# Weight units in fourths behind the last k and q tiles, five units in halves, and Sinkhorn's column sums as two 256-column products

## The chip, the cores and the metric

One core of a Trainium2 chip runs the whole program; the other cores are idle. The metric is the device time of one execution in microseconds (us), the median of several runs. TensorE (PE in the profile) multiplies matrices, VectorE (DVE), ScalarE (ACT) and GpSimd (POOL) do the rest, and SyncE (SP) issues most of the transfers. A transfer is issued by an engine's instruction stream, in the order of that stream, and moved by 16 DMA engines.

## What is computed

Three layers follow each other: a linear attention with 8 heads, a soft mixture of 8 experts with 32 slots, and a mixture of 8 experts whose gate is balanced by eight Sinkhorn steps. Everything is float32, with 2304 tokens of 512 features.

```python
# attention, per head, S = 576 rows, 128 random features
phi(x): p = x @ w_phi; p = p - max|p|;  [exp(p), exp(-p)]
num = phi(q) @ (phi(k).T @ v);  den = phi(q) @ sum(phi(k));  x = num / (den + 1e-6)
# first mixture: N = 2304 tokens, 8 experts x 4 slots, hidden 1024
slot_input = softmax(x @ phi, over tokens).T @ x
slot_out[e] = relu(slot_input[e] @ w1[e]) @ w2[e]
x = softmax(x @ phi, over slots) @ slot_out
# second mixture: 8 experts
P = exp(x @ w_gate - max)
for _ in range(8):
    P /= P.sum(1) + 1e-9
    P /= P.sum(0) + 1e-9        # the column sums: over all 2304 tokens
    P *= N / E
out = sum over e of P[:, e] * (relu(x @ w1[e]) @ w2[e])
```

## The kernel before

The tokens stand in 18 tiles of 128 rows (NT = 18). The program has three stages.

**Attention.** A loop over i runs 25 times; the k side works on tile i, the q side on tile t = i - 7. `k_project` and `q_project` multiply a k or q tile of 256 KB with w_phi and then issue the load of the tile four ahead (`load_k`, `load_q`, lines 134 and 155) on SP, into buffers of four that belong to the pools `kp` and `qtp`. From the 14th tile on there is no tile four ahead and nothing is loaded into a buffer that comes free.

**First mixture.** Its weights are 32 units of 1 MB (`units`, line 111): unit 4e + n is half n of w1 of expert e, unit 4e + 2 + n is half n of w2. In the trace and in the orders below, a unit is named by expert and half, so unit 4 is `moe_w_1_0`, unit 21 `moe_w_5_1` and unit 28 `moe_w_7_0`. Twelve units are loaded in quarters during the k loop (`attn_units`, line 495). When the k side is done its pool is closed, and in its room six more units (19 to 23 and 26) are loaded in halves by `load_part` from ACT's stream: `halves` (line 620) is the list, and each of the iterations from i = 18 takes one behind the logits and two between the exponentials. Unit 4 is loaded whole into a pool of its own (`wk1`, line 633) once the q tiles are done; units 5, 6, 10, 16 and 7 follow in halves when the q side's pool is closed (lines 678 to 682). Then the experts run in four pairs p: `up` multiplies with w1, `turn` transposes, `down` multiplies with w2. As a unit is used up its buffer takes the next load (lines 899 to 944): 17, 24, 28, 29, 25, 27, 30, 31 and the four units of the second mixture's first expert. `make_stack(0)` (line 991) is the first work that needs the last two of these.

**Second mixture.** For each expert nine blocks of 256 tokens run (`for i, (e, blk)`, line 1247). A block has 8 products of the first layer (`first_layer`) and 7 Strassen products of 12 matmuls each, all 256 columns wide; hidden values and weights are split in a rounded part and a remainder, both of the type fp32r. Beside the blocks of expert 0, `sinkhorn` (line 1021) is a generator that is advanced five times in a block: after product 1 three times, after product 5 twice. In each of its eight rounds VectorE sums P over the tiles (`cs`), TensorE sums over the partitions with one product of ones and `cs`, 8 columns wide and in float32 (line 1067, `pcs` in the trace), and VectorE divides. The column sum over the tiles is made after product 5, `pcs` runs after product 1 of the next block.

The order on each engine is the order in which the program is written (`InOrder`, line 43). Pools are stacks of memory: a pool opened where another was closed waits for the last use of the tiles it covers.

Of the kernel before, what the change touches and what calls it, by code (L numbers as in the profile page):

```python
# [54 lines left out]
def tile_kernel(ctx: ExitStack, tc: tile.TileContext, a):  # L55
# [31 lines left out]

    def w1_unit(name, e, n):
        t = unit_t[name, e, n]
        if isinstance(t, list):  # L90
            return t
        return [t[:, k * FF:(k + 1) * FF] for k in range(2)]
# [22 lines left out]
    qp = qstack.enter_context(tc.tile_pool(name="qp", bufs=2, side="left"))  # L115
    qtp_cm = tc.tile_pool(name="qtp", bufs=4, side="left")
    qtp = qtp_cm.__enter__()
    kp = kstack.enter_context(tc.tile_pool(name="kp", bufs=2, side="right"))
# [15 lines left out]
    def load_k(t):  # L134
        x = kp.tile([128, 512], F32, tag="kt", name=f"kt{t}", bufs=4)
        SP.dma_start(out=x, in_=a["kT"][t])
        kt_t[t] = x
# [48 lines left out]
    def k_project(t, banks):  # L186
        project("k", kt_t.pop(t), t, banks)
        if t + 4 < NT:
            load_k(t + 4)

# [42 lines left out]
    def q_project(t, banks):  # L233
        project("q", qt_t.pop(t), t, banks)
        if t + 4 < NT:
            load_q(t + 4)
        if t:
            q_shift(t)
# [238 lines left out]
    const.tile([128, 8], F32, name="pad", bufs=1)  # L477
# [53 lines left out]

    K0, K1, X, Q0, Q1 = "ABECD"
    for i in range(NT + LAG):
# [9 lines left out]
        if 0 <= t:  # L543
            q_num(t, 0, X)
            if i in attn_units:
                load_part(*attn_units[i], 0, 4)
            if t + 1 == NT:
                slot_dd(3, P1)
                run_exps()
                most = first.tile([128, 1, NS], F32, tag="gm", name="most", bufs=1)  # L550
                V.tensor_copy(out=most.rearrange("p o j -> p (o j)"), in_=run["mb"][:, 0:NS])
                q_divide_last(t, 0)
            q_num(t, 1, Q0)
        if i >= NT and t + 1 < NT:
            x_logits(t - 1, Q1)
        if i in attn_units:
            load_part(*attn_units[i], 1 if t >= 0 else 0, 4)
        if i >= NT and halves:
            load_part(*halves.pop(0), 2)
        if i < NT:  # L560
# [55 lines left out]
            if i + 1 == NT:  # L616
                kstack.close()
                wk_cm = tc.tile_pool(name="wk", bufs=6, side="right", reuse_waits="tile")
                wk = wk_cm.__enter__()
                halves = [(wk, u, h) for u in (19, 20, 21, 22, 23, 26) for h in range(2)]  # L620
                F0, U0, U1, P0, P1 = Q1, X, Q0, K0, K1
                X, Q0, Q1 = F0, U0, U1
# [8 lines left out]
        if t + 3 == NT:  # L631
            qtp_cm.__exit__(None, None, None)
            wk1_cm = tc.tile_pool(name="wk1", bufs=1, side="right", reuse_waits="tile")
            wk1 = wk1_cm.__enter__()
            load_units(wk1, 4)
        if t + 1 < NT:
            for hh in range(2):
                q_transpose(t + 1, hh, (F0, U1)[hh])
                q_exp(t + 1, hh)
                if halves:  # L640
                    load_part(*halves.pop(0), 2)
# [255 lines left out]
    for n in range(4):  # L897
# [3 lines left out]
        if n == 2:  # L901
            load_units(wk1, 28)
# [3 lines left out]
    for p in range(E // 2):  # L906
# [39 lines left out]
        if p == 1:  # L946
            wq_cm.__exit__(None, None, None)
            early_cm.__exit__(None, None, None)
# [8 lines left out]
    next(slot_turns)  # L957
    next(slot_splits)
    w_lo(0, 3, V)
# [10 lines left out]
    wk1_cm.__exit__(None, None, None)  # L970
    wk_cm.__exit__(None, None, None)
    wb_cm.__exit__(None, None, None)
# [48 lines left out]
    def sinkhorn():  # L1021
# [32 lines left out]
        yield  # L1054
        for it in range(8):
# [8 lines left out]
            V.tensor_reduce(out=csf, in_=P.rearrange("p t e -> p e t"), axis=AX.X, op=ALU.add)  # L1064
            yield
            pg = z_tile(0, f"pcs{it}") if it < 7 else acc_tile(f"pcs{it}")
            PE.matmul(pg[:, 0:E], ones, csf, start=True, stop=True)
# [274 lines left out]
```

## Time and profile before

| | us |
|---|---|
| median of 3 runs | 994.38 |
| lowest and highest run | 990.32, 995.48 |
| the profiled execution, its own time | 995.96 |
| span of the profile (first to last instruction) | 994.1 |

Shares of the span: PE 99 % busy, DVE 69 %, POOL 60 %, ACT 56 %. The trace gives, for each instruction, engine, start, duration and the idle time before it with what ended it. "PEld" is the loading of a matmul's stationary operand, which overlaps the matmuls. All instructions of helpers have line 51, so rows are read by the names of the tiles. Ends of matmuls are modelled: the distance between the starts of two is what they cost. A row ending in x12 merges 12 instructions.

### The profile page before, as it was taken

How to read it: one execution, taken by the hardware profiler on the slowest of the kernel's cores; microseconds unless marked ns; L12 is line 12 of the kernel's file. 1: busy time of each engine (PE TensorE's matmuls, PEld its weight loads, DVE VectorE, ACT ScalarE, POOL GpSimd, SP SyncE). 2: the span in 40 equal slices, each digit the busy share in tenths (PEclk: the TensorE clock that was granted, in tenths of full speed). 3: DMA queues.
4: the chain of work that ended last, by engine and by line, in shares of the span. 5: the costliest groups of instructions: out<-in, count | busy, mean ns of one | idle time of the engine just before them, and what ended most of it. 6: DMA issues, size and time to landing. Idle time of an engine off the chain costs nothing.

```text
span 994.1 us, 28051 instructions
## 1 busy us (share of the span) xinstructions
PE 980.6 (99%) x11698; PEld 935.7 (94%) x11698; DVE 688.8 (69%) x1360; ACT 556.5 (56%) x1018; POOL 593.7 (60%) x462
## 2 busy tenths in 40 slices
PE   8899999999999999999999999999999999999998
PEld 7899987569999999999999999999999999999998
DVE  6778766277886766676766776676676677667675
ACT  5566554265657666655564555554654565555452
POOL 2122220055678677867786678678777777787443
PEclk9999999999999999999999999999999999999999
DMA  8777578980003100310040004000400130001111
GB/s 238 219 239 221 170 244 301 393 303 2 1 1 128 44 1 1 128 44 2 1 156 16 1 1 170 2 2 20 151 2 1 66 106 1 2 1 38 49 44 64
DMA packets 29517, 88.84 MB, mean 89 GB/s; under 512 B 3920, under 2 KB 6864, under 8 KB 24144
## 3 DMA queue, kind: packets, MB, share of 16 engines
q1 hardware_dynamic: 20560, 68.05, 20.0%
q10 hardware_dynamic: 8640, 18.88, 5.9%
q8 instruction: 92, 1.51, 0.6%
q14 instruction: 33, 0.27, 0.1%
q0 software_dynamic: 192, 0.13, 0.1%
HBM read 82.33 MB, written 4.72 MB: 88 GB/s over the span
## 4 chain that ended last, share of the span: by engine, by line
PE 96%; DMA 1%; DVE 1%; issue 1%; ACT 1%; DVEq 0%; ACTq 0%
PE x L51 39%; PE y L51 20%; PE z L51 16%; PE kvacc L51 4%; PE num L51 3%; PE pq L51 2%; PE pk L51 2%; PE ut L51 2%; DMA moe_w<-in_moe_w 1%; PE ps L51 1%; PE ph L51 1%; PE po L51 1%; PE xt L51 1%; PE lg L51 1%; PE xl L51 1%
## 5 line engine op out<-in xcount | busy, mean ns | idle before, releaser
L51 POOL TENSOR_TENSOR hl_s<-s,hh_s 128x512 fp32r<-128x512 f32 x286 | 365.5, 1300 | 205.7 <-ACT hh_s L51 189.6
L51 PE MATMUL x<-w_t,hh_s 128*128 128x256 f32 x1152 | 204.7, 278 | 0.1
L51 ACT ACTIVATE hh_s<-s 128x512 fp32r<-128x512 f32 x287 | 174.9, 630 | 50.6 <-PE x L51 26.3
L51 ACT ACTIVATE r<-z 128x512 f32<-128x512 f32 x143 | 85.8, 600 | 163.0 <-PE z L51 162.3
L51 PEld LDWEIGHTS x<-w_t,hh_s 128*128 128x128 f32 x1152 | 173.4, 188 | 1.1 <-ACT xo L51 0.3
L51 DVE SCALAR_TENSOR_TENSOR xo<-x,P,xo 128x256 f32<-128x256 f32 x252 | 120.9, 480 | 68.3 <-PE x L51 66.7
L51 ACT ACTIVATE hh_a<-z 128x512 fp32r<-128x512 f32 x216 | 122.2, 600 | 73.2 <-DVE s L51 71.7
L51 PE MATMUL x<-w_t,hl_s 128*128 128x256 f32 x576 | 158.7, 276 | 0.0
L51 DVE SCALAR_TENSOR_TENSOR s<-z,r 128x512 f32<-128x512 f32 x143 | 98.0, 685 | 84.6 <-ACT hh_a L51 80.7
L51 DVE SCALAR_TENSOR_TENSOR hl_a<-z,hh_a 128x512 fp32r<-128x512 f32 x216 | 147.1, 681 | 2.7 <-ACT hh_a L51 2.7
L51 PEld LDWEIGHTS x<-w_t,hl_s 128*128 128x128 f32 x576 | 107.9, 188 | 0.0
L51 PE MATMUL z<-w_b,hh_a 128*128 128x256 f32 x576 | 102.4, 278 | 0.0
L51 PE MATMUL y<-w_b,hh_s 128*128 128x256 f32 x576 | 101.7, 276 | 0.0
L51 PE MATMUL x<-w_t,hh_a 128*128 128x256 f32 x576 | 101.6, 276 | 0.0
L51 PE MATMUL y<-w_t,hh_s 128*128 128x256 f32 x576 | 101.6, 276 | 0.0
L51 PE MATMUL x<-w_b,hh_a 128*128 128x256 f32 x576 | 101.3, 276 | 0.0
L51 DVE SCALAR_TENSOR_TENSOR s<-z,s 128x512 f32<-128x512 f32 x143 | 97.7, 684 | 3.9 <-POOL hl_s L51 2.1
L51 PEld LDWEIGHTS z<-w_b,hh_a 128*128 128x128 f32 x576 | 86.6, 188 | 2.9 <-issue 2.9
L51 PEld LDWEIGHTS y<-w_b,hh_s 128*128 128x128 f32 x576 | 86.8, 188 | 0.0
L51 PEld LDWEIGHTS x<-w_t,hh_a 128*128 128x128 f32 x576 | 86.8, 188 | 0.0
L51 PEld LDWEIGHTS y<-w_t,hh_s 128*128 128x128 f32 x576 | 86.8, 188 | 0.0
L51 PEld LDWEIGHTS x<-w_b,hh_a 128*128 128x128 f32 x576 | 86.6, 188 | 0.0
(211 smaller groups left out, 1982.7 us busy)
## 6 DMA issues: line engine op xcount, KB each, us to landing
moe_w<-in_moe_w SPq DMA_DIRECT2D x41, 1024.0 KB, 6.9
moe_w<-in_moe_w ACTq DMA_DIRECT2D x48, 256.0 KB, 3.7
moe_w<-in_moe_w ACTq DMA_DIRECT2D x12, 512.0 KB, 5.3
vs<-in_vb SPq DMA_DIRECT2D x20, 256.0 KB, 4.2
kt<-in_kT SPq DMA_DIRECT2D x18, 256.0 KB, 4.1
qt<-in_qT SPq DMA_DIRECT2D x18, 256.0 KB, 3.4
half<-in_moe_w SPq DMA_DIRECT2D x8, 512.0 KB, 6.6
out<-xo SPq DMA_DIRECT2D x18, 128.0 KB, 1.7
```

Source lines behind the costliest of these rows:

```text
L51: return lambda *args, **kwargs: self.tc.keep_in_program_order(make(*args, **kwargs))
```

## The change

It has three parts.

- **Weight units.** The k tiles get a pool of their own (`ktp`) that stays open, and the pool of the q tiles (`qtp`) moves below the q side's and stays open too. Behind the last four k tiles come the four fourths (256 KB each) of unit 4, behind the last four q tiles the fourths of unit 21, and later, in the same buffers as unit 4, the fourths of unit 28. All are issued by SP. `Columns` makes two fourths look like one tile. The pool `wk1` is gone, `wk` has 5 buffers instead of 6, and `halves` holds five units (20, 19, 22, 23, 26), taken four times per iteration instead of three.
- **Column sums.** VectorE rounds `cs` to fp32r (`csh`) and takes the remainder (`gst`), and TensorE multiplies ones of the type fp32r with both, each repeated 32 times to 256 columns, in one accumulation.
- **One VectorE instruction.** `w_lo(0, 3, V)` stands ahead of the last `slot_splits` instead of behind it.

```diff
+    def load_fourth(pool, tag, u, m):
+        name, e, n = units[u]
+        t = pool.tile([128, 512], F32, tag=tag, name=f"{name}_{e}_{n}_{m}")
+        SP.dma_start(out=t, in_=a[name][e, :, n * 2048 + m * 512:n * 2048 + (m + 1) * 512])
+        unit_t.setdefault(units[u], []).append(t)
...
-    qp = qstack.enter_context(tc.tile_pool(name="qp", bufs=2, side="left"))
     qtp_cm = tc.tile_pool(name="qtp", bufs=4, side="left")
     qtp = qtp_cm.__enter__()
+    qp = qstack.enter_context(tc.tile_pool(name="qp", bufs=2, side="left"))
+    ktp_cm = tc.tile_pool(name="ktp", bufs=4, side="right")
+    ktp = ktp_cm.__enter__()
...
         if t + 4 < NT:
             load_k(t + 4)
+        else:
+            load_fourth(ktp, "kt", 4, t + 4 - NT)
...
         if t + 4 < NT:
             load_q(t + 4)
+        else:
+            load_fourth(qtp, "qt", 21, t + 4 - NT)
...
+        if i >= NT:
+            load_next()
         if i >= NT and t + 1 < NT:
             x_logits(t - 1, Q1)
...
-        if i >= NT and halves:
-            load_part(*halves.pop(0), 2)
+        if i >= NT:
+            load_next()
...
-                wk_cm = tc.tile_pool(name="wk", bufs=6, side="right", reuse_waits="tile")
+                wk_cm = tc.tile_pool(name="wk", bufs=5, side="right", reuse_waits="tile")
                 wk = wk_cm.__enter__()
-                halves = [(wk, u, h) for u in (19, 20, 21, 22, 23, 26) for h in range(2)]
+                halves = [(wk, u, h) for u in (20, 19, 22, 23, 26) for h in range(2)]
...
-        if t + 3 == NT:
-            qtp_cm.__exit__(None, None, None)
-            wk1_cm = tc.tile_pool(name="wk1", bufs=1, side="right", reuse_waits="tile")
-            wk1 = wk1_cm.__enter__()
-            load_units(wk1, 4)
...
         if n == 2:
-            load_units(wk1, 28)
+            for m in range(4):
+                load_fourth(ktp, "kt", 28, m)
...
     next(slot_turns)
+    w_lo(0, 3, V)
     next(slot_splits)
-    w_lo(0, 3, V)
...
+        onesr = cp.tile([128, 128], F32R, tag="onesr", name="onesr")
+        V.tensor_copy(out=onesr, in_=ones)
         for it in range(8):
...
             V.tensor_reduce(out=csf, in_=P.rearrange("p t e -> p e t"), axis=AX.X, op=ALU.add)
+            V.tensor_copy(out=csh, in_=csf)
+            V.tensor_tensor(out=gst, in0=csf, in1=csh.bitcast(F32), op=ALU.subtract)
             yield
             pg = z_tile(0, f"pcs{it}") if it < 7 else acc_tile(f"pcs{it}")
-            PE.matmul(pg[:, 0:E], ones, csf, start=True, stop=True)
+            for n in range(2):
+                PE.matmul(
+                    pg[:, 0:256].rearrange("p (r e) -> p r e", r=32), onesr,
+                    (csh, gst)[n].unsqueeze(1).to_broadcast([128, 32, E]), start=n == 0, stop=n == 1,
+                )
```

TensorE, in an early block of expert 0, between product 1 (`z`) and product 2 (`x`), before and then after:

```order
L51 MATMUL z_5199<-w_b_3993,hl_a_6_5113 128x256
L51 MATMUL pcs_5213<-cs_5164,ones 128x8
L51 MATMUL x_5185<-w_t_4035,hh_s_6_5133 128x256 x2
L51 MATMUL x_5185<-w_t_4035,hl_s_6_5135 128x256
L51 MATMUL x_5185<-w_t_4035,hh_s_6_5133 128x256 x2
```

```order
L51 MATMUL z_4756<-w_b_4010,hl_a_3_4668 128x256
L51 MATMUL pcs_4770<-csh,onesr 128x256
L51 MATMUL pcs_4770<-gst,onesr 128x256
L51 MATMUL x_4742<-w_t_4052,hh_s_3_4688 128x256 x2
L51 MATMUL x_4742<-w_t_4052,hl_s_3_4690 128x256
```

The one float32 product of 8 columns has become two fp32r products of 256; nothing else moved there.

SP, at the end of the k and q loads (`qt` are tiles of q, `half` the halves of units 5, 6, 10 and 16), before and then after:

```order
L51 DMA qt_2289<-in_qT 128x512
L51 DMA qt_2474<-in_qT 128x512
L51 DMA qt_2661<-in_qT 128x512
L51 DMA qt_2813<-in_qT 128x512
L51 DMA qt_2915<-in_qT 128x512
L51 DMA moe_w_1_0_3394<-in_moe_w 128x2048
L51 DMA half_3610<-in_moe_w 128x1024
```

```order
L51 DMA qt_2296<-in_qT 128x512
L51 DMA moe_w_1_0_2_2324<-in_moe_w 128x512
L51 DMA qt_2483<-in_qT 128x512
L51 DMA moe_w_1_0_3_2511<-in_moe_w 128x512
L51 DMA qt_2672<-in_qT 128x512
L51 DMA qt_2824<-in_qT 128x512
L51 DMA qt_2927<-in_qT 128x512
L51 DMA moe_w_5_1_0_3047<-in_moe_w 128x512
L51 DMA moe_w_5_1_1_3166<-in_moe_w 128x512
L51 DMA moe_w_5_1_2_3276<-in_moe_w 128x512
L51 DMA moe_w_5_1_3_3396<-in_moe_w 128x512
L51 DMA half_3620<-in_moe_w 128x1024
```

Unit 4, which stood whole between the last q tile and the first half, has gone up among the q tiles in fourths, and unit 21, which ACT issued, has come in fourths to its place.

VectorE, at the end of the first mixture (`cst` is the split of the slot weights, `w_t` and `w_b` remainders of the second mixture's weights), before and then after:

```order
L51 TENSOR_TENSOR w_t_4035<-t_3965,w_t_4035 128x1024
L51 CAST cst_4068<-lg 128x2x32 x2
L51 TENSOR_TENSOR cst_4068<-lg,cst_4068 128x2x32 x2
L51 TENSOR_TENSOR w_t_3995<-moe_w_0_0_3896,w_t_3995 128x1024
L51 TENSOR_TENSOR moe_w_0_0_3896<-moe_w_0_0_3896,moe_w_0_1_3898 128x4x256
```

```order
L51 TENSOR_TENSOR w_t_4052<-t_3982,w_t_4052 128x1024
L51 TENSOR_TENSOR w_t_4012<-moe_w_0_0_3912,w_t_4012 128x1024
L51 CAST cst_4086<-lg 128x2x32 x2
L51 TENSOR_TENSOR cst_4086<-lg,cst_4086 128x2x32 x2
L51 TENSOR_TENSOR moe_w_0_0_3912<-moe_w_0_0_3912,moe_w_0_1_3914 128x4x256
```

The remainder `w_t` of line 959 now stands ahead of the last split instead of behind it.

## Rows read from the trace of the kernel before

**Rows 1.** Stretches: start:end, length, PE, PEld, DVE, ACT, POOL busy, PEclk, DMA share, GB/s.
```profile
170.00:215.00 45.00, 43.01 (x559) 23.88 (x549) 19.76 (x62) 16.56 (x30) 8.11 (x9) 1.00 0.92 356
215.00:310.00 95.00, 94.61 (x832) 92.64 (x831) 77.21 (x152) 58.45 (x121) 66.33 (x45) 1.00 0.11 41
310.00:988.00 678.00, 678.00 (x6077) 670.07 (x6076) 467.24 (x897) 379.30 (x642) 484.27 (x321) 1.00 0.13 43
```

**Rows 2.** Chain of work, one piece: start us, us, what.
```profile
195.64 14.71 DMA moe_w<-in_moe_w
```

**Rows 3.** Timeline of PE, 207 to 211: start, us, engine, out<-in, count [idle <-releaser].
```profile
207.85 1.07 PE L51 MATMUL ps<-moe_w,sot 128*32 128x256 f32 x16 [0.28 <-DMA moe_w<-in_moe_w]
208.85 0.69 PE L51 MATMUL pgate<-wg,sot 128*64 128x64 f32 x16
210.40 1.07 PE L51 MATMUL ps<-moe_w,sot 128*32 128x256 f32 x16 [0.87 <-DMA moe_w<-in_moe_w]
```

**Rows 4.** Chain of work: product 6 with the next block's product 0.
```profile
237.10 2.83 PE x L51 x24
...
302.11 2.72 PE x L51 x24
...
326.08 2.72 PE x L51 x24
336.50 2.72 PE x L51 x24
```

**Rows 5.** Timeline of PE: three column sums of expert 0 and the next product.
```profile
230.12 0.28 PE L51 MATMUL pcs<-cs,ones 128*128 128x8 f32 x2
...
241.18 0.29 PE L51 MATMUL pcs<-cs,ones 128*128 128x8 f32 x2
241.32 0.48 PE L51 MATMUL x<-w_t,hh_s 128*128 128x256 f32 x2
...
251.85 0.28 PE L51 MATMUL pcs<-cs,ones 128*128 128x8 f32 x2
```

**Rows 6.** Timeline of DVE: gate rounding, the first column sum, the last split.
```profile
206.05 0.30 DVE L51 CAST cst<-lg 128x64 fp32r<-128x64 f32 x2 [1.22 <-PE pc L51]
...
209.97 0.16 DVE L51 CAST gst<-pgate 128x8 fp32r<-128x8 f32 x1
210.16 0.17 DVE L51 TENSOR_TENSOR gst<-pgate,gst 64x8 fp32r<-64x8 f32 x1
...
228.85 0.43 DVE L51 TENSOR_REDUCE cs<-P 128x8 f32<-128x144 f32 x1
```

**Rows 7.** Transfers of unit 4: issue (count, ns, when) and time to landing.
```profile
L51 SPq DMA_DIRECT2D moe_w<-in_moe_w x1: 328/328/328, 154.7 to 154.7; - x1
...
DMA to landing us min/median/max: 5.1/5.1/5.1
```

**Rows 8.** The same for one half, issued at 161.7.
```profile
L51 SPq DMA_DIRECT2D half<-in_moe_w x1: 327/327/327, 161.7 to 161.7; - x1
...
DMA to landing us min/median/max: 4.6/4.6/4.6
```

**Rows 9.** The same for the last unit before `make_stack(0)`.
```profile
L51 SPq DMA_DIRECT2D moe_w<-in_moe_w x1: 328/328/328, 195.6 to 195.6; - x1
...
DMA to landing us min/median/max: 14.7/14.7/14.7
```

**Rows 10.** Stretches by DMA: columns as in Rows 1.
```profile
105.00:130.00 25.00, 25.00 (x705) 23.58 (x695) 20.35 (x42) 16.10 (x38) 5.39 (x12) 1.00 0.56 171
135.00:150.00 15.00, 14.61 (x341) 13.14 (x338) 10.62 (x27) 9.06 (x25) 4.14 (x8) 1.00 0.91 300
180.00:205.00 25.00, 24.98 (x304) 11.01 (x296) 9.56 (x24) 8.07 (x13) 3.19 (x6) 1.00 1.01 420
205.00:210.00 5.00, 4.25 (x53) 2.82 (x48) 3.95 (x8) 3.11 (x7) 0.00 (x0) 1.00 0.47 149
```

**Rows 11.** Timeline of ACT at 130: logits copied, then a half issued.
```profile
130.00 0.19 ACT L51 COPY lg<-lg 128x32 f32<-128x32 f32 x1 [0.25 <-PE lg L51]
130.01 0.33 ACTq L51 DMA_DIRECT2D moe_w<-in_moe_w  x1
```

More of the change, by code (lines that the diff above doesn't have):

```diff
@@ L86, in load_part, with __init__, __getitem__ @@
         A.dma_start(out=unit_t[units[u]][:, r], in_=a[name][e, :, n * 2048:(n + 1) * 2048][:, r])
+    def load_fourth(pool, tag, u, m):
[3 more added lines that the diff above has]
+        unit_t.setdefault(units[u], []).append(t)
+    class Columns:
+        def __init__(self, tiles):
+            self.tiles = tiles
+        def __getitem__(self, at):
+            p, c = at
+            return self.tiles[c.start // 512][p, c.start % 512:c.start % 512 + c.stop - c.start]
     def w1_unit(name, e, n):
         t = unit_t[name, e, n]
+        if isinstance(t, list) and len(t) == 4:
+            return [Columns(t[0:2]), Columns(t[2:4])]
         if isinstance(t, list):
@@ L134, in load_k @@
     def load_k(t):
-        x = kp.tile([128, 512], F32, tag="kt", name=f"kt{t}", bufs=4)
+        x = ktp.tile([128, 512], F32, tag="kt", name=f"kt{t}")
         SP.dma_start(out=x, in_=a["kT"][t])
@@ L476, in tile_kernel @@
     load_k(3)
-    const.tile([128, 8], F32, name="pad", bufs=1)
+    csh = const.tile([128, E], F32R, name="csh", bufs=1)
     wg = const.tile([128, KC, E], F32, name="wg", bufs=1)
@@ L530, in slot_rest, with load_next @@
                 slot_norm(g, t - 4 * g - 7)
+    def load_next():
+        if halves:
+            load_part(*halves.pop(0), 2)
     K0, K1, X, Q0, Q1 = "ABECD"
@@ L639, in tile_kernel @@
                 q_exp(t + 1, hh)
-                if halves:
-                    load_part(*halves.pop(0), 2)
+                load_next()
             x_turn(t)
@@ L947, in tile_kernel @@
             wq_cm.__exit__(None, None, None)
+            qtp_cm.__exit__(None, None, None)
             early_cm.__exit__(None, None, None)
@@ L969, in tile_kernel @@
     keep_busy(True, 2)
-    wk1_cm.__exit__(None, None, None)
     wk_cm.__exit__(None, None, None)
+    ktp_cm.__exit__(None, None, None)
     wb_cm.__exit__(None, None, None)
```

## The prediction

> **What bounds the kernel now.** I read the stretches first. From 310 to 988 us TensorE is busy without a gap, from 215 to 310 all but 0.4 of 95 us, and from 170 to 215 it misses 2 us of 45 [rows 1]. So TensorE sets the time nearly everywhere. A change of transfers is worth only the TensorE waits that it takes away, and a change of TensorE's own work is worth what that work costs in the stream of matmuls. I therefore looked for two things: where TensorE waits for a transfer, and what the column sums cost it.
>
> The chain of waits has one long piece that is a transfer, 14.7 us that end when `make_stack(0)` can go on [rows 2]. The chain is followed back from the last link, so this is not 14.7 us of idle TensorE. The timeline of TensorE tells what it is worth: the two halves of `make_stack(0)` waited 0.28 and 0.87 us for their weight units, and between them there was work [rows 3]. Together 1.15 us: no more can be won from weights here, since ahead of it TensorE had its transposes and products to do.
>
> The column sums show in the distance of equal pieces. From 326.08 to 336.50 one block of a later expert takes 10.42 us. From 237.10 to 302.11 six blocks of expert 0 take 65.01 us, 10.835 each [rows 4]. The only work in a block of expert 0 that later blocks don't have is one `pcs`, so **each column sum costs 0.415 us**, though its two records start within 0.14 us [rows 5]. The starts of successive sums tell why: 11.06 us from the first to the second, 10.67 from the second to the third [rows 5]. After the one sum all following matmuls come at a slower pace until the next, after the other they don't. I call the two the slow and the fast pace; they differ by 0.39 us a block. A block has 84 + 8 = 92 matmuls, so the fast pace is 10.42 / 92 = 0.113 us each and the slow one 0.39 / 92 = 4 ns more. The granted clock is 1.00 throughout, that is its level of 2.4 GHz [rows 1], so the clock is not the cause. In the fast period the sum itself costs 10.67 - 10.42 = 0.25 us.
>
> **Column sums.** Removed: eight sums of 0.415 us, 3.3 us. Added: sixteen products of 256 columns, of the form that all others in the block have, at 0.113 us: 1.8 us. If the pace stays fast, the gain is 1.5 us. The end below is this value. The end above is a pace that is slow through all eight blocks, which nothing in them would then correct, since no float32 matmul is left there: each block 10.42 + 0.39 + 2 x 0.118 = 11.05 us against 10.835, that is 0.21 us more, and 1.7 us slower in eight. I take the fast pace, because it is what a block with nothing but 256-column products of these types shows [rows 4].
>
> VectorE gets two small instructions a round, priced by the same pair on the gate, 0.16 + 0.17 us [rows 6], and once a copy of ones. In round 0 the column sum starts at 228.85 and lasts 0.43 us, so it is ready at 229.28; `pcs` starts at 230.12 [rows 5, 6]. With 0.33 us, and the copy ahead of it at no more than 0.30 us (the pair of casts of half its width, [rows 6]), the operands are ready at 229.9. That is still 0.2 us ahead. In other rounds there is a little more. So I cost it at nothing. The cover is that margin; if it is gone, TensorE waits some 0.1 to 0.3 us once, in round 0.
>
> A rule weighed against this. The trace shows 0.25 us for a float32 sum of 8 columns even at the fast pace, more than the 0.227 us of two 256-column products. The Trainium skill, "TensorE: Matmul & The Clock Gate", section "Back-to-back issue gap", gives about 60 cycles to a matmul of up to 64 columns and 262 cycles to one of 256; by it two records would be 0.05 us, the new pair 0.22 us, and eight rounds an estimated 1.4 us slower. The trace does not agree: 0.25 us stand in the place of that 0.05.
>
> **Weight units.** Unit 4 leaves its place at 154.67 us, where it landed in 5.1 us [rows 7], and goes among the q tiles at some 85 to 115 us, where the DMA engines are busy by 0.56 [rows 10]. Unit 21 moves from ACT to SP within the same ten microseconds or so. The five other units are issued some 8 us earlier, since four halves go per iteration; between 135 and 150 us the DMA engines are already busy by 0.91 at 300 GB/s [rows 10], so they are queued longer rather than done much earlier. Behind these transfers on ACT stands the copy of the logits, which was ready 0.25 us after ACT came free [rows 11]; one more issue takes 0.33 us [rows 11], so the copy can be some 0.1 us late, ahead of work of TensorE that has slack from the second such iteration on. I cost it at nothing, at most 0.3 us. On SP, the fourths wait for the k or q tile before them, as all tiles did, and the tiles of v behind them are issued later in any case; the halves from 155 us on come after the last fourth, and were waiting for the q side's buffers.
>
> What does it do for the last unit, issued at 195.64 and landed at 210.36 [rows 9]? The transfers are saturated there: 1.01 busy at 420 GB/s from 180 to 205 [rows 10]. It counts only what was still queued at 174 us, when the first pair's buffers came free. A half issued at 161.7 landed in 4.6 us, less than unit 4 alone had needed [rows 7, 8]: by then unit 4 was out of the way, and the queue of 174 us was built by the halves behind. So moving unit 4 may do nothing there. The end below is that both waits go: -1.15 us. The end above comes from unit 28, which is now moved in fourths, in rows of 2 KB as the tiles of k, q and v, in the middle of the saturated stretch. Where such rows and quarters prevail, the engines move 171 / 0.56 = 305 GB/s per full share, in the saturated stretch 420 / 1.01 = 416 [rows 10]; 1.05 MB then take 3.4 instead of 2.5 us, and the last unit is 0.9 us later. The Trainium skill, "DMA: Bandwidth & Descriptors", section "Bandwidth", asks for transfers of 1 MiB and more; the direction is the same, and the sum doesn't need it. Between -1.15 and +0.9 I take 0: rows 8 is the nearest row, and says that the backlog that matters is built later than unit 4.
>
> **The moved VectorE instruction** fills a gap of 1.22 us ahead of the last split, in which VectorE waited for transposes [rows 6]. What follows on VectorE, and the weight parts on ACT and POOL behind it, comes 1.2 us earlier. TensorE waits for none of it: next on its path is the weight unit [rows 3]. Worth 0, and cover for the case that the unit comes earlier.
>
> Sum: -1.5 + 0 + 0. On the profiled execution, 995.96 us, that is 994.5; on the median of the runs, 994.38, which lies 1.6 below, **992.9 us**. A difference under 0.5 %, some 5 us, is about what a measurement of this kernel can tell from no change; the runs before spread by 5.2.
>
> **The rivals.**
> 1. *Slow pace.* The new products leave TensorE in the slow pace for the whole of expert 0: +1.7 instead of -1.5, 996.1 us. For it: the pace of the trace changes with nothing but `pcs` and holds until the next. Against it: all later experts run fast. Chance 0.2.
> 2. *The sums become dearer.* If a small float32 sum occupied TensorE only for the 0.14 us between its start and the next product's [rows 5], the new pair would cost 0.227 - 0.14 = 0.09 us more, 0.7 in eight: 995.1 us. Against it: 0.25 us missing even in a fast period. The rule of the Trainium skill above points here. Chance 0.1.
> 3. *Slower than before.* The pace that expert 0 leaves is carried over `make_stack` into later experts. Each expert has nine blocks, 9 x 0.39 = 3.5 us. One such expert stays under 5 us; from two on it decides: -1.5 + 7.0, 999.9 us, with all seven some 1017. Against it: the blocks of 310 to 988 us are all fast in the trace, after an expert 0 that had both paces. Chance 0.07.
> 4. *The transfers do what they are for.* Both waits go: -1.5 - 1.15, 991.7 us. For it: 1 MB less behind 155 us; against it rows 8. Chance 0.25, within the forecast's range.
>
> **How the numbers follow.** Forecast with the transfers at 0 or somewhat off: 0.38, and with rival 4, 0.63. Ends: -1.5 - 1.15 gives 991.7, +1.7 + 0.9 gives 997.0. Three runs before lay from 4.1 under to 1.1 over their median, and the median of three moves by about half of that; so I take 989.5 to 997.0. Rival 3 and odd draws stay outside. Faster by over 0.5 % would be under 989.4, which only a draw like the lowest run before gives: 0.06. Slower by over 0.5 %: rival 3, 0.07. Within: 0.87.
>
> **What would show it.** Right: blocks of expert 0 at 10.65 us and none at 11.05; the chain still ends in the last unit at some 210 us. Slow pace: blocks at 11.05 throughout. Dearer sums: more than 0.23 us between product 1 and 2 beyond a later block. Rival 4: no idle time of `make_stack(0)` for a transfer. Wrong altogether: a new wait of TensorE for transfers or exponentials between 85 and 170 us, or later blocks off 10.42.

## The result, and the profile after

The changed kernel is slower. Its median is **1005.42 us** (six runs, 1000.93 to 1006.15) against 993.88 of the kernel before (six runs, 990.32 to 995.48): a ratio of **1.0105, interval 1.0085 to 1.0125**. The forecast was 992.9 us with a range up to 997.0, so both the value and the range missed. The profiled execution took 1005.61 us with a span of 1003.4; the span before was 994.1, so the two traces differ by 9.3 us.

The start of the first `z` product of each expert divides both traces into stages:

| stage | before, us | after, us | difference |
|---|---|---|---|
| start to the first `z` of expert 0 | 213.74 | 215.27 | +1.5 |
| expert 0 (eight rounds of Sinkhorn beside it) | 96.64 | 102.35 | +5.7 |
| expert 1 | 96.74 | 96.78 | 0 |
| expert 2 | 96.73 | 98.96 | +2.2 |
| rest of the span | 490.3 | 490.0 | -0.3 |

Three stages changed; I take the largest first.

**Expert 0.** The two later stretches of [rows 1] in the changed kernel, with the same columns:

```profile
215.00:310.00 95.00, 91.91 (x769) 89.92 (x769) 81.20 (x156) 55.69 (x116) 62.63 (x43) 1.00 0.09 36
310.00:988.00 678.00, 677.63 (x6069) 668.31 (x6068) 467.25 (x900) 380.90 (x645) 485.25 (x322) 1.00 0.13 44
```

From 215 to 310 us TensorE had 0.4 us of idle time before; now it has 3.1. What it waits for, 220 to 320 us (waits of TensorE: who waits, for whom, us in total, times, longest):

```profile
PE pcs L51 <- DVE gst L51: 2.1, 6, 0.6
PE pcs L51 <- DVE csh L51: 0.6, 1, 0.6
```

Neither line existed before: TensorE waits for the two small VectorE instructions that the prediction cost at nothing. All eight of each, grouped by form (min/median/max in ns, first and last start):

```profile
L51 DVE CAST csh<-cs x8: 171/682/684, 232.1 to 311.7; 128x8 fp32r<-128x8 f32 x8
L51 DVE TENSOR_TENSOR gst<-cs,csh x8: 168/1199/1206, 232.3 to 312.4; 128x8 fp32r<-128x8 f32 x8
```

The shortest of each takes the 0.17 us that I had read from [rows 6]; the median takes **0.68 and 1.20 us**, for 8 elements per partition. One block shows why: the timeline of all engines from 241.5 to 244.5 us (start, us, engine, instruction):

```profile
241.53 2.58 POOL L51 TENSOR_TENSOR hl_s<-s,hh_s 128x512 fp32r<-128x512 f32 x2 [0.76 <-DVE s L51]
...
242.23 0.66 DVE L51 CAST csh<-cs 128x8 fp32r<-128x8 f32 x1
...
242.93 1.21 DVE L51 TENSOR_TENSOR gst<-cs,csh 128x8 fp32r<-128x8 f32 x1
...
243.61 0.28 PE L51 MATMUL pcs<-csh,onesr 128*128 128x256 f32 x1
...
244.19 0.38 PE L51 MATMUL pcs<-gst,onesr 128*128 128x256 f32 x1 [0.30 <-DVE gst L51]
```

GpSimd's record covers two equal instructions, 241.53 to 242.86 and from there to 244.11. `csh` ends at 242.89 and `gst` at 244.14, each a few hundredths after one of them. All fourteen long ones of this trace end so, 0.02 to 0.03 us behind an `hl_s` of GpSimd. They don't compute for that long; they are held until GpSimd has finished. TensorE's second `pcs` then starts 0.58 us behind the first, where two such products are 0.12 apart: 0.46 us lost in this block, in the same way in the next ones.

The Trainium skill, "SBUF — State Buffer", section "Who interferes with whom", says that a VectorE instruction with two SBUF inputs contends with a GpSimd instruction that reads SBUF, that a cast can do so too in one of its modes, and that the one that comes second is blocked until the other has ended. These rows agree, with 0.17 against 0.68 and 1.20 us.

**The pace.** The blocks of expert 0, from `z` to `z`, take 11.64, 11.62, 11.62, 11.58, 11.53 and 11.58 us; before they took 11.03 or 10.71. Taking off 0.46 leaves 11.1, which is the slow pace of [rows 5] in *every* block. The chain of waits shows it by the length of pieces of 12 products (start, us, what):

```profile
258.54 1.41 PE y L51 x12
...
339.67 1.36 PE y L51 x12
```

1.41 us is the slow pace and 1.36 the fast one, here in expert 0 and in expert 1.

**Start to the first z.** The wait for the last weight units shrank as rival 4 said: `ps` waits 0.21 us once, against 0.28 and 0.87 in [rows 3], and the last unit landed in 13.9 us instead of 14.7 [rows 9]. But more was lost earlier. Chain of waits of the changed kernel, then of the kernel before, at the same matmuls:

```profile
147.01 0.15 PE xl L51 x5
147.16 1.67 issue
...
149.70 1.92 PE pq L51 x32
151.62 1.72 PE ut L51 x8
```

```profile
146.11 0.15 PE xl L51 x5
146.26 0.39 issue
...
147.52 1.03 PE pq L51 x32
148.55 1.02 PE ut L51 x8
```

Two things differ. After the fifth `xl` TensorE stands still for 1.67 us instead of 0.39 and waits for nothing that the profile shows ("issue"). And the 32 `pq` and 8 `ut` products behind it take 1.92 and 1.72 us instead of 1.03 and 1.02. The stretches there tell why (length; PE, PEld, DVE, ACT and POOL busy; PEclk; DMA share; GB/s):

```profile
146.00:148.00 2.00, 1.16 (x41) 1.11 (x36) 0.79 (x3) 1.44 (x5) 0.00 (x0) 1.00 1.02 396
148.00:150.00 2.00, 1.17 (x21) 1.08 (x24) 0.26 (x1) 0.19 (x1) 1.19 (x2) 0.90 0.25 95
150.00:152.00 2.00, 2.00 (x34) 1.67 (x27) 0.37 (x2) 0.00 (x0) 0.00 (x0) 0.50 0.04 8
152.00:154.00 2.00, 2.00 (x22) 1.83 (x22) 1.86 (x4) 1.24 (x3) 0.00 (x0) 0.74 0.42 128
```

The granted clock falls to 0.50 (1.2 GHz) after the stop and is back at 2.4 GHz some 3 us later. The stop costs 1.28 us and the clock 1.59; two smaller stops ahead of it, at 136 and 141 us, cost 0.9. The shorter wait for the units gives back 0.94, and a stop of the kernel before at 172.6 us, worth 1.1, is gone. Such stops stand in both traces from 17 us on, at changing places: those of over 0.25 us add up to 5.4 us ahead of the first `z` before and to 5.3 after. So the two traces don't show more stops in all, but a longer one here and a lower clock behind it. What the stops are comes below, in "The stop and the clock".

**Expert 2.** Its first three blocks take 10.55, 10.42 and 10.43 us; the fourth takes 10.74, and from there on they take 10.83. It turns at 450.79, in the middle of the fourth with no column sum, no float32 product and no recorded wait near:

```profile
450.45 0.39 PE L51 MATMUL y<-w_b,hh_s 128*128 128x256 f32 x2
...
450.79 0.50 PE L51 MATMUL x<-w_t,hh_a 128*128 128x256 f32 x2
...
451.24 0.40 PE L51 MATMUL x<-w_t,hh_a 128*128 128x256 f32 x2
...
451.60 0.40 PE L51 MATMUL x<-w_t,hh_a 128*128 128x256 f32 x2
```

Three products take 0.34 us up to 450.79 by the starts of these rows, the next three 0.45, and the three behind them 0.36. What turned it shows only beside the other traces, in "What neither half shows".

### The profile page after: what moved, and what is told of

Read it like the earlier page. It is cut to its first block, busy times and chain, and to the rows that moved or that the text cites. A ratio compares the mean times of both kernels' runs of the same rounds, so it can differ in the third digit from the quotient of the medians.

```text
span 1003.4 us, 28087 instructions
## 1 busy us (share of the span) xinstructions
PE 986.9 (98%) x11698; PEld 939.9 (94%) x11698; DVE 698.6 (70%) x1377; ACT 556.7 (55%) x1018; POOL 594.0 (59%) x462
## 4 chain that ended last, share of the span: by engine, by line
PE 90%; POOL 3%; DVE 3%; issue 2%; DMA 1%; ACT 1%; POOLq 0%; DVEq 0%; ACTq 0%
PE x L51 36%; PE y L51 18%; PE z L51 15%; PE kvacc L51 4%; PE num L51 3%; POOL hl_s L51 2%; PE pq L51 2%; PE pk L51 2%; PE ut L51 2%; DMA moe_w<-in_moe_w 1%; PE ph L51 1%; PE ps L51 1%; PE po L51 1%; DVE gst L51 1%; PE xl L51 1%
## 5 line engine op out<-in xcount | busy, mean ns | idle before, releaser
L51 PE MATMUL y<-w_t,hh_s 128*128 128x256 f32 x576 | 102.0, 277 | 0.0
```

The lines of the kernel that those rows point to most:

```text
L51: return lambda *args, **kwargs: self.tc.keep_in_program_order(make(*args, **kwargs))
```

## The experiments

The theory after this reading: **the split on VectorE is held by GpSimd; TensorE waits for it, and the slow pace comes with these waits.** The first rival: the wide products themselves cost time or leave the slow pace. The second: the weight units cause most of it. Times are medians; ratios are to the kernel before on the same chip, whose medians were 994.4 to 995.4.

### The two halves of the change apart

The kernel before with the new sums alone, `sums_only` (diff to the kernel before; the pair of products is as in the change):

```diff
+            V.tensor_copy(out=csh, in_=csf)
+            V.tensor_tensor(out=gst, in0=csf, in1=csh.bitcast(F32), op=ALU.subtract)
             yield
...
-            PE.matmul(pg[:, 0:E], ones, csf, start=True, stop=True)
+            for n in range(2):
```

> The kernel before with the new column sums alone; weights as before. Theory: the two small VectorE instructions, which read two SBUF operands while GpSimd is in one of its own, last until GpSimd ends (0.68 and 1.20 us in the changed kernel instead of 0.17), TensorE waits for them, and every wait leaves it in the slow pace. Then nearly all of the loss is here: blocks of expert 0 at 11.6 us, the first layer of expert 1 some 5.7 us later than before, 999.5 to 1002 us in all. Rival, that the transfers cost it: 993 to 995 us, blocks of expert 0 at 10.65.

Measured: 999.86 us, 1.0046 (1.0026 to 1.0066). Expert 0 takes 102.0 us, its blocks 11.49 to 11.60; `csh` and `gst` have medians of 0.68 and 1.20 us, and TensorE waits 2.9 and 0.6 us for them. Expert 2 stays fast. Expert 0 takes 5.3 us more than before, so nearly all of its 5.7 us in the change belong to the sums alone.

The changed kernel with the old sums, `units_only`:

```diff
-            V.tensor_copy(out=csh, in_=csf)
-            V.tensor_tensor(out=gst, in0=csf, in1=csh.bitcast(F32), op=ALU.subtract)
...
+            PE.matmul(pg[:, 0:E], ones, csf, start=True, stop=True)
```

> The changed kernel with the old column sums: only the weight units and the moved remainder. Theory: the four halves per iteration fill the DMA engines when TensorE needs its next instructions, it stops for 1.67 us at 147 us instead of 0.39 and its clock falls to the lower level for some 3 us; against it 1 us less of waiting for the last weight units. Net +1 to +2.5 us, 995 to 996.5. Rival, that the transfers cost most of the loss: 1000 us or more. Rival, that the stop was chance: 992.5 to 993.5.

Measured: 997.39 us, 1.0033 (1.0014 to 1.0052), somewhat more than expected. The blocks of expert 0 are those of before. The stop is there (1.40 us at 149.29), and behind it the granted clock is 0.58 and 0.56 for 4 us. The units cost a third of a per cent, nothing of it in the second mixture.

### Is it the split or the wide products?

The reduction writes its rounded result itself, and both products take that, so the products stay and the split goes (`sums_nosplit`, diff to `sums_only`; the remainder is left out and the sum is taken twice, so only the time is read):

```diff
-            V.tensor_reduce(out=csf, in_=P.rearrange("p t e -> p e t"), axis=AX.X, op=ALU.add)
-            V.tensor_copy(out=csh, in_=csf)
-            V.tensor_tensor(out=gst, in0=csf, in1=csh.bitcast(F32), op=ALU.subtract)
+                V.tensor_reduce(out=csh, in_=P.rearrange("p t e -> p e t"), axis=AX.X, op=ALU.add)
...
-                    (csh, gst)[n].unsqueeze(1).to_broadcast([128, 32, E]), start=n == 0, stop=n == 1,
+                    csh.unsqueeze(1).to_broadcast([128, 32, E]), start=n == 0, stop=n == 1,
```

> The kernel before with the two 256-column products, but VectorE's reduction writes the rounded sum itself and both products take it: the two small instructions are left out, and with them the remainder (the sum is taken twice, so P comes out halved in each round). Theory: TensorE then waits for nothing at the sums, and blocks of expert 0 are 10.65 us (fast pace, 991.5 to 993.5 us in all) or 11.05 (slow pace, 995 to 997). Rival, that the wide products themselves cost it: blocks stay at 11.5, 999 to 1001 us.

Measured: 996.54 us, 1.0014 (1.0001 to 1.0027); expert 0 takes 96.9 us, as before. Its blocks: 11.06, 11.02, 10.65, 10.72, 10.65, 10.71. The fast block with two wide products is the 10.65 us that the prediction had worked out. Chain of waits around one of the pairs:

```profile
250.01 1.41 PE z L51 x12
251.42 0.22 PE pcs L51 x2
251.65 1.38 PE x L51 x12
253.02 0.91 PE z L51 x8
253.93 1.36 PE y L51 x12
```

The pair costs 0.22 us, and at this pair the pace turns from 1.41 to 1.36 us for 12 products. The first rival falls: the wide products neither cost more than their columns nor keep the slow pace. That the time is still not below that of before has a place in the trace: expert 4 takes 98.13 instead of 96.73 us, slow from its sixth block on. It belongs to "What neither half shows".

The other way round, the split is made and not used (`split_unused`, diff to the kernel before):

```diff
+            V.tensor_copy(out=csh, in_=csf)
+            V.tensor_tensor(out=gst, in0=csf, in1=csh.bitcast(F32), op=ALU.subtract)
             yield
             pg = z_tile(0, f"pcs{it}") if it < 7 else acc_tile(f"pcs{it}")
             PE.matmul(pg[:, 0:E], ones, csf, start=True, stop=True)
```

> The kernel before with the two small VectorE instructions added, whose results nothing uses; the old float32 product stays. Theory: the two last 0.68 and 1.20 us as in the changed kernel, but the old product waits only for the sum; VectorE has room, so blocks of expert 0 stay near 10.7 and 11.05 us as the pace has it, 994 to 996 us. Rival, that the time VectorE loses is itself the loss: 998 us and more.

Measured: 997.30 us, 1.0029 (1.0014 to 1.0043), again more than expected. VectorE's instructions by form:

```profile
L51 DVE CAST csh<-cs x8: 668/674/679, 228.8 to 304.3; 128x8 fp32r<-128x8 f32 x8
L51 DVE TENSOR_TENSOR gst<-cs,csh x8: 167/1204/1211, 229.5 to 305.1; 128x8 fp32r<-128x8 f32 x8
```

The instructions are held as long as in the changed kernel, but no `pcs` waits, and the blocks are 10.70 to 11.03, apart from 0.46 us more in the last: expert 0 takes 97.2 us. The long instructions hurt because a product stands behind them, not by themselves. Its span is 1.3 us over that of before, and the trace places that: 1.4 us are in expert 6, which takes 98.15 instead of 96.73 us, slow from its sixth block on, and 0.5 in expert 0; the first `z` comes 0.6 earlier.

### Out of GpSimd's way

Two attempts to move the split to where GpSimd reads nothing. First, all of a round behind product 1 (`sums_early`, diff to `sums_only`):

```diff
-    SINK = {1: 3, 5: 2}
+    SINK = {1: 5}
```

> sums_only with all five steps of a round after product 1, where GpSimd sits idle for 3.4 us, instead of two of them after product 5. Theory of the shared access: the two small instructions fall to 0.17 us each, TensorE waits for none of them, blocks of expert 0 are 11.05 us at the slow pace or 10.65 at the fast, 3.5 to 7 us less than sums_only, 993 to 998 us. Rival, that VectorE simply has too much to do: the same work is there, blocks stay at 11.4 or more.

Measured: 1002.33 us, 1.0081 (1.0058 to 1.0103). VectorE's instructions by form:

```profile
L51 DVE CAST csh<-cs x8: 171/171/173, 226.6 to 302.8; 128x8 fp32r<-128x8 f32 x8
L51 DVE TENSOR_TENSOR gst<-cs,csh x8: 166/168/169, 226.8 to 303.0; 128x8 fp32r<-128x8 f32 x8
L51 DVE TENSOR_TENSOR P<-P,cs x8: 309/2098/2276, 227.9 to 315.0; 128x144 f32<-128x144 f32 x8
```

The mechanism is confirmed: in another place, with no instruction of GpSimd beside them, the same two instructions take 0.17 us, all sixteen of them. The time isn't won, and that expectation missed. Now `P<-P,cs` collides with GpSimd's `w_b` (one ends 0.2 us behind the other at 241 us) and takes 2.1 us, with the rest of the round and the block's own work queued behind it on VectorE; TensorE waits 5.0 us, in six waits, for an `xo` among these. Waits of TensorE:

```profile
PE x L51 <- DVE xo L51: 5.0, 6, 2.2
```

Part of the loss is the clock. The last block of expert 0 takes 17.5 us instead of 13.4. TensorE was busy for 1.81 of the 4 us from 302 on, and behind that the granted clock is 0.58 from 306 to 310 us. There 24 products take 4.61 us (chain of waits), where [rows 4] has 2.83:

```profile
305.57 4.61 PE x L51 x24
```

Second, the last two steps behind product 4 instead of 5 (`sums_k4`, diff to `sums_only`):

```diff
-    SINK = {1: 3, 5: 2}
+    SINK = {1: 3, 4: 2}
```

> sums_only with the row scaling and the column sum after product 4 instead of after product 5, so that the remainder is ready some two products earlier. Theory: VectorE is still held by GpSimd for about the same time, but TensorE waits for neither operand; blocks 11.05 us at the slow pace, 10.65 at the fast; 994 to 997 us. Rival, that VectorE's lost 1.5 us is what counts, not the wait of the column sum: another wait takes its place, blocks at 11.4 or more, 998 us and more.

Measured: 1010.17 us, 1.0163 (1.0134 to 1.0192), the slowest of all. `csh` is free (0.17 us), `gst` is still held (1.21), and a new wait is on top, for `xo`, which ACT makes (waits of TensorE):

```profile
PE x L51 <- ACT xo L51: 5.1, 6, 1.3
PE pcs L51 <- DVE s L51: 1.8, 5, 0.4
```

Here too the granted clock falls, to 0.59 from 304 to 308 us, behind the longest of these waits. A step of VectorE can't be put anywhere in the block for free; the old place was the best of the three tried.

### The stop and the clock

Four halves per iteration could be what fills the DMA engines and stops the instruction stream. The edit to `units_only` is one such pair of lines for three halves (`units_three`), and two for two halves (`units_two`):

```diff
-        if i >= NT:
-            load_next()
```

> The same with three halves per iteration as in the kernel before (the take ahead of the logits is left out). If the crowding of the halves makes the stop, it shrinks to 0.2 to 0.6 us, the clock stays at 1.00 between 145 and 160 us, and the time is 2 to 3 us below units_only, 992.5 to 994. If the place of the fourths on SP makes it, the stop stays above 1 us.

> units_only with two halves per iteration, both between the exponentials, so that the five units are spread over five iterations. Theory of the crowded transfers: the DMA engines move under 350 GB/s where TensorE needs its instructions behind the fifth product of the logits near 147 us, it stops there for under 0.6 us, the clock stays at 1.00, and the time is that of the kernel before or up to 1 us less, 993 to 994.5 us. Rival, that the fourths on SP cost it: stop over 1 us, 996 us and more.

Measured: 996.68 us with three, 1.0017 (1.0002 to 1.0032), and 994.14 with two, 0.9991 (0.9973 to 1.001). With three the expected gain missed: the stop has another place (1.22 us at 141.01), while the clock stays at 1.00; with two there is neither from 125 to 170 us. (Ahead of that `units_two` has stops too, the longest 1.83 us at 26.58, with no fall of the clock.) The kernel before with four halves per iteration (`before_four`):

```diff
+        if i >= NT and halves:
+            load_part(*halves.pop(0), 2)
```

> The kernel before with four halves per iteration instead of three, all else as it was. Theory of the crowded transfers: TensorE stops for over 1 us for its instructions between 140 and 155 us, and its granted clock falls below 0.9 for some us behind; 1 to 3 us slower, 995 to 997 us. Rival, that these stops are chance: no fall of the clock, 993.5 to 994.5 us.

Measured: 995.92 us, 1.0014 (0.9998 to 1.0029). Three stops, 0.60 us at 137.08, 1.00 at 142.96 and 0.57 at 149.44, but no fall of the clock: that expectation missed. The units alone, unchanged, once more (`units_again`):

> A second look at units_only. If the stop near 147 us comes from the crowding, it is over 1 us again, the DMA engines move 400 GB/s or more in the four us around its start, and the clock falls behind it. If it was chance: under 0.6 us and no fall.

Measured: one run, 1001.26 us; stop 1.94 us at 147.64, granted clock 0.50 from 150 to 156. The chain of waits there:

```profile
147.49 0.15 PE xl L51 x5
147.64 1.94 issue
```

Ahead of the stop the DMA engines are full in two of the three traces with a clock that falls behind it: busy by 1.03 in the changed kernel (143 to 147 us, 416 GB/s) and in `units_only` (409 GB/s), but 0.94 in `units_again` (328 GB/s, where the expectation wanted 400). So the busy share alone doesn't tell. The packets of the traces do. The changed kernel's page has two queues that move instructions (packets, MB, share of the 16 engines):

```profile
q8 instruction: 92, 1.51, 0.6%
q14 instruction: 34, 0.28, 0.1%
```

The packets of q8 have 16 KB each, and their number fits TensorE's 23,711 records in blocks of 256. The 17 traces have 65 stops of over 0.5 us in the chain of waits from 10 to 210 us. Counted over all of TensorE's records, from 0, all 65 stand at number 193 or a multiple of 256 behind it, the one at 147 us at 193 + 29 x 256. TensorE goes on 1.0 to 1.6 us (median 1.4) after the block of q8 for that place has landed: in the changed kernel the block is moved from 146.34 to 147.38 and TensorE goes on at 148.83, in `units_again` from 147.22 to 148.14 and at 149.58. **So the stop is TensorE waiting for its next 256 instructions.**

The halves make the block late. In the stretch of the halves (the blocks asked for between 124 and 150 us) the latest one starts 2.5 to 3.1 us after TensorE has passed the place before, in the three kernels with two halves per iteration; 2.2 to 4.3 us in the nine with three; 4.4 to 5.1 us in the five with four. In the second mixture, where the DMA engines are busy by 0.13, a block starts at the median 0.9 us ahead of that place. With five microseconds from one place to the next, four halves leave a stop of over 0.5 us in every trace there, three in some, two in none. Why the clock falls behind some stops and not behind others of the same length is not shown.

The Trainium skill, "Runtime: NRT & Kernel Launch", section "Instruction fetch mechanics", says that engines fetch their instructions by a DMA queue of their own, in blocks of 256, mostly hidden. The traces agree on the queue and on TensorE's 256; with stops of up to 1.94 us it isn't hidden here.

### Who sets the pace?

In the kernel before, a throwaway product stands ahead of block 0 of each later expert. Without it (`before_bare`):

```diff
-        if n and e and blk == 0:
-            for _ in range(1):
-                PE.matmul(z[:, 0:256], stacks[e][:, 120:248], ct[0][:, 120:376], start=True, stop=True)
```

> The kernel before without the one throwaway product of 256 columns that precedes the first layer of experts 1 to 7. If the pace is a state that the number or timing of instructions sets and that lasts until the next disturbance, the blocks of experts 1 to 7 come at 10.82 us instead of 10.42, some 25 us more, 1015 to 1021 us. If the pace belongs to the float32 products alone, the blocks stay at 10.42 us and the time is 0.8 us less.

Measured: one run, 998.16 us, between the two expectations. Expert 1 runs at 10.83 us in every block, 3.4 us more for the expert; experts 2 to 7 at 10.43, and their first blocks also take 10.43 instead of 10.55. So the slow pace outlives expert 0, as rival 3 supposed, and can hold a whole expert; here with no float32 product in it; and the throwaway product is needed once, not seven times. Chain of waits, expert 1 and then expert 2:

```profile
311.03 1.41 PE y L51 x12
312.44 1.41 PE x L51 x12
...
411.15 1.36 PE y L51 x12
412.51 1.36 PE x L51 x12
```

Does such a product help behind the column sums? One more 256-column product behind the pair (`sums_third`, diff to `sums_only`):

```diff
+            PE.matmul(pg[:, 256:512], onesr, ct[0][:, 120:376], start=True, stop=True, skip_group_check=True)
```

> sums_only with one throwaway product of 256 columns behind each pair. If such a product turns the pace, the part of each block behind it comes at 0.34 us per three products instead of 0.353: blocks 11.5 + 0.11 - 0.35, 11.25 us, 997 to 999 us. If not, blocks are 11.6 to 11.7 us, 1000 to 1001 us.

Measured: one run, 999.52 us; blocks 11.60 to 11.74, all slow. It doesn't turn the pace while TensorE waits for the split (2.6 and 0.6 us here).

### What neither half shows

Sums and units alone cost 0.46 and 0.33 per cent, together 0.79; the change costs 1.05. The intervals nearly close that gap, but the traces name a difference of 2.2 us: expert 2, which is fast in both. The changed kernel once more (`after_again`), and with two halves per iteration (`after_two`, the edit of `units_two`):

> The changed kernel once more, beside the next two on one chip. Theory that the parts add up: 0.46 % for the sums and 0.33 % for the weight units, 0.8 % slower, 1002 to 1003.5 us; the stop near 147 us over 1 us again, with the lower clock behind it. If the two parts make each other worse: 1.0 % or more, 1005 us.

> The changed kernel with two halves per iteration, both between the exponentials. Theory: the stop and the low clock go, the sums' loss stays with blocks of expert 0 at 11.5 to 11.6 us; 0.35 to 0.5 % slower than before, 998 to 1000 us. If the two parts make each other worse, it stays above 1002 us.

Measured: 1005.62 us, 1.0094 (1.0065 to 1.0124), and 1004.29, 1.0090 (1.0058 to 1.0122). In both, expert 2 turns slow in the same block as in the first trace (10.74 or 10.75 us, then 10.83 to its end): that is all three traces with both halves of the change, and none of `sums_only`, `sums_third` and the `units_` kernels. It isn't the transfers' rate, since two halves per iteration took the stop near 147 us away and left this. In `after_again` the stops are 0.58 us at 136.32 and 1.28 at 142.19, and the clock does not fall: it is still 1 per cent slower than before, so the first stage isn't the main part.

The trigger in expert 2 is in VectorE's rows, in the block that turns. The changed kernel, and then the kernel before, where this block starts 7.28 us earlier:

```profile
448.06 0.69 DVE L51 SCALAR_TENSOR_TENSOR s<-z,r 128x512 f32<-128x512 f32 x1 [1.57 <-ACT hh_a L51]
...
450.25 0.48 DVE L51 SCALAR_TENSOR_TENSOR xo<-x,P,xo 128x256 f32<-128x256 f32 x1
```

```profile
440.43 0.69 DVE L51 SCALAR_TENSOR_TENSOR s<-z,r 128x512 f32<-128x512 f32 x1 [1.23 <-ACT hh_a L51]
...
442.63 0.47 DVE L51 SCALAR_TENSOR_TENSOR xo<-x,P,xo 128x256 f32<-128x256 f32 x1
```

`s` comes 0.35 us late, with nothing to wait for but what had come, and VectorE's row behind it is late with it. The `xo` ends 0.06 us ahead of the product that turns (450.79), where before it ended 0.41 us ahead; the next product follows 0.22 us later instead of 0.11. The same late `s` turns expert 4 in `sums_nosplit` (653.74 us), expert 6 in `split_unused` (848.49) and expert 5 in `sums_k4` (795.26), and none of these has the weight units. These six are the only ones of 1,071 blocks (experts 1 to 7, 17 traces) in which `s` is late, and but for `before_bare` the only ones in which a later expert turns slow.

Counted over all of VectorE's records, the late `s` has the number 831, 1215, 1471 or 1599: always 63 and a multiple of 128. The packets of q14 have 8 KB, half of TensorE's, and 34 of them are about what the 4,376 records of VectorE, ACT, GpSimd and SyncE need in blocks of 128. So a late `s` is the first of a block of instructions, by all that the traces show. Which instruction that is depends on how many VectorE has had before: in `sums_only` the same `s` is number 829, in `units_only` 814. The 2.2 us are no work of either half, but a place in the stream that the two together moved.

### A version that beats both

The units in two halves per iteration, the old sums, and the throwaway product for expert 1 alone (`two_bare`, diff to `units_two`):

```diff
-        if n and e and blk == 0:
+        if n and e == 1 and blk == 0:
```

> The kernel with the weight units early, two halves per iteration, the old column sums, and the throwaway product kept for expert 1 alone. Its blocks of expert 1 should be 10.42 us, and the first blocks of experts 2 to 7 10.43 instead of 10.55: 0.7 us less than units_two, 992.5 to 994.5 us, not to be told from the kernel before. If the pace of a later expert depends on the product after all, 3.6 us more for each such expert.

Measured: **992.93 us, 0.9977 (0.9959 to 0.9995)**, span 990.1. All later blocks take 10.42 to 10.43 us, the first of experts 2 to 7 included. The first blocks are worth 6 x 0.12 = 0.7 us against `units_two`. Of the 4.1 us between the two spans (994.2 and 990.1) 3.4 are an earlier first `z`, 210.73 against 214.10, with the same attention in both: this start lies anywhere from 209.7 to 216.5 us in the traces without a fall of the clock ahead of it, with stops at changing places. So what is sure of the gain over `units_two` is the 0.7 us; the intervals of the two kernels overlap.

## Why the prediction was wrong

- **The step that failed: the price and the cover of the split.** "Priced by the same pair on the gate, 0.16 + 0.17 us", with 0.2 us to spare. The gate's pair reads its input from PSUM, and its second instruction (210.16) took 0.17 us although a GpSimd instruction with two SBUF inputs ran beside it, in the kernel before:

```profile
210.08 2.36 POOL L51 TENSOR_TENSOR w_t<-moe_w,w_t 128x1024 fp32r<-128x1024 f32 x1 [5.97 <-ACT w_t L51]
```

  The new pair reads SBUF beside `hl_s`. It took 0.68 + 1.20 us in nearly every round, 1.5 us more than priced, and TensorE lost about 0.46 us a block. The cover of 0.2 us was that of round 0 alone; the "little more" of the other rounds is 1.15 to 1.45 us in the trace of before (from the end of `cs` to `pcs`), so the price of 0.33 us was covered there and the measured one was not. The prediction names 0.1 to 0.3 us once if the cover is gone, but neither end of its range has them. The trace of before had the warning, in an instruction I didn't look at: the division by the column sums, with the same shape as the one by the row sums, varies from 0.3 to 2.3 us (the kernel before, by form):

```profile
L51 DVE TENSOR_TENSOR P<-P,cs x8: 309/1986/2267, 231.2 to 309.5; 128x144 f32<-128x144 f32 x8
```

  At 242.22 it takes 1.99 us and ends with GpSimd's `w_b` (241.62 and 2.41 us). A duration with a wide spread, on an instruction of fixed size, was a price list for VectorE instructions beside GpSimd in this stretch.
- **The copy of ones** was bounded at 0.30 us and took 0.85 (at 229.38); in round 0 TensorE waits 0.6 us for `csh`. It is probably the same error in small: two `hl_s` of GpSimd ran from 228.84 to 231.48.
- **Pace.** The fast pace was chosen; the slow one, rival 1, came in all blocks. The size of the step was right, 0.39 us a block. Its reason as I put it ("no float32 matmul is left there" to correct it) fell: without the split the same wide products do turn the pace (`sums_nosplit`). What the changed kernel, `sums_only` and `sums_third` share is a wait of TensorE for the split in all but one or two blocks; that this wait resets the pace is the likeliest reading, not tested by itself. The six turns in later experts, each at a product that came 0.11 us late, point the same way. Why the fast pace comes back at some products and not at others stays open.
- **The wide products** cost what was predicted: 0.22 us a pair, 10.65 us a block. The saving of 1.5 us was not seen even there: in `sums_nosplit` the six blocks take 64.8 instead of 65.2 us, two of them slow, and the first block, with one wait of 0.4 us for `csh`, is 0.7 longer.
- **Weight units, cost 0 between -1.15 and +0.9.** Rival 4 came true with 0.94 of its 1.15 us. What was left out is a stop of TensorE ahead of 150 us, 1.28 us longer, in which its next instructions were late behind the halves, and a lower clock behind it, 1.59. The prediction did look at that stretch and its full DMA engines [rows 10], but only asked how long transfers queue, not what TensorE does.
- **Four halves per iteration, "at most 0.3 us".** Wrong place: the copy of the logits was not what mattered. Two halves instead of four took the ratio from 1.0033 to 0.9991, some 4 us.
- **Rival 3** came near by luck. A later expert did run slow, 2.2 us in expert 2, but the pace was not carried over from expert 0: expert 1 is fast, and expert 2 turns in its fourth block. That a pace can be carried into expert 1 only `before_bare` shows. The slower result came from the sums.
- **The moved VectorE instruction** stayed at 0: nothing on TensorE's path waits there in either trace.

## What to carry to other kernels

Price a new VectorE instruction by one that reads the same memory beside the same work of GpSimd, and read the spread of a group (minimum, median, maximum) before its mean: the minimum is the work, the rest is waiting. An instruction that is cheap by itself is dear if a matmul stands behind it with less time to spare than it can be held (here 1.15 to 1.45 us), and moving it changes whom it blocks. Where TensorE runs without gaps, also compare equal pieces of it (12 products in 1.36 or 1.41 us): a wait can cost more than its length. And look through all of a trace before a loss is put down to the edit: here a few more instructions on VectorE moved the start of an instruction block, and a stage that the edit doesn't touch lost up to 2.2 us.

## What the runs showed of the hardware that I had not expected

- An instruction of 8 elements per partition took 0.17, 0.68 or 1.20 us, by what GpSimd did beside it.
- The same stream of 256-column products runs at two paces at the same granted clock of 1.00: 10.43 or 10.83 us a block. The pace holds over whole experts (`before_bare`), and in six traces it turned at a product that came 0.11 us late.
- TensorE's instructions come in blocks of 256 as packets of 16 KB. While the weights were loading, a block started up to 5.1 us after the place before it, and TensorE stood still for up to 1.94 us with nothing to wait for in the profile; in three traces the granted clock fell to 0.50 behind such a stop near 147 us, for 3.4 to 6.8 us.
- In six traces an instruction of VectorE, each a multiple of 128 records behind number 63, came 0.35 us late with nothing to wait for, and TensorE's pace turned behind it.
